# A parallel FNet and gated layer in split fp32: the odd block and the rest rows of the last stage join the 2x2 scheme as a twelfth pair

## The chip, the cores and the metric

The kernel runs on one core of one Trainium2 chip. The metric is the time of one execution on the device, in microseconds (us). Three runs of the kernel before gave a median of 1033.83 us (1033.81 to 1034.27).

## What is computed

The reference, cut to what matters (S = 2048 tokens, D = 640, F = 1728, all fp32):

```python
xn = _layernorm(x, axis=-1)
# A: FNet mixing
a = einsum("bsd,ed->bse", xn, dft_hid_re);  b = einsum("bsd,ed->bse", xn, dft_hid_im)
A = einsum("ts,bse->bte", dft_seq_re, a) - einsum("ts,bse->bte", dft_seq_im, b)
# B: gated layer
gate = einsum("bsd,df->bsf", xn, W_gate);  up = einsum("bsd,df->bsf", xn, W_up)
h = where(gate > 0, gate, 0) * up
return x + A + einsum("bsf,fd->bsd", h, W_down)
```

## The kernel before, in words

Every fp32 operand is split into a high part (a copy rounded to the fp32r format, by ScalarE) and a low part (the rest, by VectorE; `split`, L123), and every product of two operands is made of three matmuls, high x high, high x low and low x high, into one PSUM bank (`mm3`, L127).

The kernel has three stages. In the first, the sequence transforms of the normalized tokens are made first (the order of the two transforms in A is exchanged), as partial products P and Q that go to DRAM (`pqd`). In the second, 26 rounds (`gate_up`, 13 blocks of 128 columns of F for each half of the tokens, some 12 us a round) make h and store it to DRAM (`hd`, 13 blocks of 128 rows for each half; `hrest`, the 64 rows that are left, since 1728 = 13 x 128 + 64). In rounds 13 to 23, `pair_weights` (L945) prepares beside that the weights of the last stage and stores them in DRAM as `wparts`. The third stage, `project` (L1038), which the change is about, adds everything up: out = x + hid x (P, Q) + W_down x h, transposed, so that 128 outputs stand in the partitions and 512 tokens in the columns.

The last stage runs over two halves of the tokens (q = 1, then 0), each of two chunks of 512 tokens. A half's product is made by a 2x2 scheme of seven products instead of eight (Strassen's scheme in Winograd's form): the inner dimension is cut into pairs of 128-row blocks, the outputs into pairs of blocks (0, 1 against 2, 3; the fifth block of outputs goes along in the products that allow it), the tokens into the two chunks. The seven products of a half follow each other in the order B11, T1, B21, T2, B22, T3, T4. The T's take differences of the loaded chunks as moving operand (VectorE makes them, L1092 to L1104) and prepared sums as weights. B11, T1, B21 and B22 write three output tiles each, T2, T3 and T4 two: 18 tiles. Each product runs over 11 pairs of blocks in six units: h0, h1 (two pairs each) and h2 (one pair) over the hidden dimension (P against Q), f0, f1, f2 (two pairs each) over blocks 0 to 11 of h. So a unit of two pairs is 18 matmuls in a product with three tiles, and 12 in one with two. A product's result is read out of its PSUM banks by VectorE, which adds it to a tile y (`add_y`, L1192); y starts as x, loaded by L1190, and goes to DRAM when its last product has been added. T2, T3 and T4 add to the banks "a" of the products before them: B11 writes a, T2 adds, T3 adds, T4 adds, with a read after each.

Block 12 of h and the 64 rest rows do not make a pair. Before the change they are done by plain products (`plain_block` L1128, `plain_rest` L1147, `plain_run` L1174): ten tiles in a half, each by three matmuls for block 12 and two for the rest rows, which stand twice in the partitions, so that one matmul does two of the three partial products. They run behind B21 and B22 (three tiles each) and behind T3 (two tiles of banks "o" of their own, then two of the banks a).

The order of the work: units are entered in a list `todo` of (load, prepare, run, finish) and `drive(4, 2)` (L701) walks through it: a unit's loads are issued four entries ahead of its matmuls, its splits two ahead, its read one behind. Loads are all issued from SP's queue in this order, so a load that waits holds up every load behind it; output stores are issued by GpSimd's queue, except the last ones. The pools set the waits: `ring2` (3 buffers for the split moving operand), `wraw` (4 raw weight tiles), `wts` (5 split weight tiles; for T2, T3 and T4 the loads go right into these, L1075), `raws` (24 raw chunks of 4 KB in a partition; each lives until the last product that needs it), `plain`, and `y` (ten tiles of 2 KB). The pools are opened where the ones of the earlier stages were closed (L1035), some from the left and some from the right end of the memory, and a new tile waits for the tiles that lay in its place.

The first unit of the stage (h0 of B11, q = 1) is made ahead, so that TensorE goes over without a break: its operands are loaded by `lead_load` and split by `lead_split` into a tile of the second stage's weight pool gw1 (L989 to L1000), which also held the weights of the last round. This is the lead unit; in the profile its matmuls are `ps<-gw`. Its raw chunk is loaded once more into `raws` (L1068 and L1069), as T1 needs it. In the profile `rw` is a raw chunk, `wr` a raw weight tile, `cb` a split chunk, `wt` a split weight tile, `pw` the tile of `pair_weights`, and `hp`, `hr`, `wp`, `wq`, `pr` are the plain products' tiles.

Of the kernel before, what the change touches and what calls it, by code (L numbers as in the profile page):

```python
# [7 lines left out]
F32 = mybir.dt.float32  # L8
# [43 lines left out]
NPAIR = KD + NF // 2  # L52
# [6 lines left out]
def fnet_reglu_kernel(  # L59
# [885 lines left out]
    def pair_weights(k, n):  # L945

        t = {}

        def load():
            t["z"] = z = pool("prep").tile([P, Y12 + 2 * P], F32, name="pw")  # L950
            wa, wb = pair(k, 1)
            for w, o1, o2 in ((wa[0], Y11, Y21), (wb[0], Y12, LOW + Y22)):
                nc.sync.dma_start(z[:, o1 : o1 + 2 * P], w[:, : 2 * P])
                nc.sync.dma_start(z[:, o2 : o2 + 2 * P], w[:, 3 * P :])

        def prepare():
# [3 lines left out]
            tt(zz(LOW + Z2), zz(Z1), zz(Y11), op=OP.subtract)  # L960
            tt(zz(LOW + Z3), zz(Y11), zz(Y21), op=OP.subtract)
            tt(zz(Z4), zz(Y12), zz(LOW + Z2), op=OP.subtract)

            high, src = z[:, HIGH:LOW], z[:, LOW:NW]
            split(high.bitcast(F32R), src, src)

        loads[n - 1].append(load)
        besides[n].append(prepare)
        issues[n + 1].append(lambda: nc.gpsimd.dma_start(wparts[:, k], t["z"][:, :NW]))

    def pair(k0, n):

        if k0 < KD:
            return hid[0, k0 : k0 + n], hid[1, k0 : k0 + n]
        f = 2 * (k0 - KD)
        w = wd[f * P : (f + 2 * n) * P].rearrange("(k i p) n -> k i p n", i=2, p=P)
        return w[:, 0], w[:, 1]
# [57 lines left out]
    for n, b, side in (("wraw", 4, "left"), ("ring2", 3, "left"), ("wts", 5, "left"), ("raws", 24, "left"), ("plain", 1, "right"), ("y", 1, "right")):  # L1035
        open_pools[n] = ctx.enter_context(tc.tile_pool(name=n, bufs=b, side=side, reuse_waits="tile"))

    def project(q):  # L1038
        c0, c1 = 2 * q, 2 * q + 1
        units = [("hid", u) for u in HID_UNITS] + [("f", u) for u in F_UNITS]  # L1040
        raws, B, y, plain = {}, {}, {}, {}

        def get(kind, u):
            what, ks = units[u]
            o = raws[kind, u] = pool("raws").tile([P, 2, CH], F32, name="rw")[:, : len(ks)]
            col, row = int(kind in ("B12", "B22")), int(kind in ("B21", "B22"))
            if what == "hid":
                nc.sync.dma_start(o, pqd[(c0, c1)[col]][row][:, ks[0] : ks[-1] + 1])
            else:
                nc.sync.dma_start(o, hd[q][2 * ks[0] + row : 2 * ks[-1] + row + 1 : 2, :, col * CH : (col + 1) * CH].rearrange("f p t -> p f t"))  # L1050

        def unit(name, u, first):
            what, ks = units[u]
            n, k0 = len(ks), ks[0] + (KD if what == "f" else 0)
# [3 lines left out]
            def load():  # L1058
# [6 lines left out]
                ahead = {("B21", 1): 0, ("B21", 3): 1, ("B21", 5): 2, ("T2", 0): 3, ("T2", 2): 4, ("T2", 3): 5}.get((name, u))  # L1065
# [4 lines left out]
                own, sums = [i.rearrange("k p n -> p k n") for i in pair(k0, n)], wparts[:, k0 : k0 + n]  # L1070
                if name in PARTS:
                    t["w"] = w = weights()
                    for j in range(n):
                        at = sums[:, j, HIGH:].rearrange("p (v n) -> p v n", v=2)[:, :, PARTS[name] : PARTS[name] + 2 * P]
                        nc.sync.dma_start(w[:, j, :, : 2 * P].bitcast(F32), at)  # L1075
                    return
# [8 lines left out]
            def prepare():  # L1085
# [5 lines left out]
                with in_turn():  # L1091
# [3 lines left out]
                    elif name == "T2":  # L1095
                        src = r("B12")
                        sub(src, r("B22"), src)
                    elif name == "T3":
                        src = r("B11")
                        sub(src, r("B12"), src)  # L1100
                    elif name == "T4":

                        src = r("B21")
                        sub(src, src, r("B12"))  # L1104
# [3 lines left out]
                    lows.append(split(b[:, 0], b[:, 1], src))  # L1108
                    if "r" in t:
# [3 lines left out]
            def run():  # L1113
# [5 lines left out]
                for out, oo, more in [((key, i), o + i * P, more) for i in range(2)] + ([(row4[1], row4[0], name in ("B21", "B22"))] if row4 else []):  # L1119
                    if first and not more:  # L1120
                        B[out] = bank()
                    for j in range(n):
                        mm3(B[out], (w[:, j, 0, oo : oo + P], w[:, j, 1, oo : oo + P]), (b[:, 0, j], b[:, 1, j]),
                            first and not more and j == 0, u == len(units) - 1 and j == n - 1, more)

            return load, prepare, run

        def plain_block():  # L1128


            def load():
                plain["r"] = r = pool("plain").tile([P, W2 + D], F32, name="pr")
                nc.sync.dma_start(r[:, :W2], hd[q][NF - 1])
                if q == 1:
                    nc.sync.dma_start(r[:, W2:], wd[(NF - 1) * P : NF * P])

            def prepare():
                r = plain["r"]
                plain["h"] = h = pool("plain").tile([P, 2, W2], F32R, name="hp")
                split(h[:, 0], h[:, 1], r[:, :W2])  # L1140
                if q == 1:
                    PW["w"] = w = pool("plain").tile([P, 2, D], F32R, name="wp")
                    split(w[:, 0], w[:, 1], r[:, W2:])

            todo.append((load, prepare, idle, idle))

        def plain_rest():  # L1147


            def load():  # L1150
                plain["r2"] = r = pool("plain").tile([P, W2 + D], F32, name="pr")
                for i in range(2):
                    at = slice(i * REST, (i + 1) * REST)
                    nc.sync.dma_start(r[at, :W2], hrest[q])
                    if q == 1:
                        nc.sync.dma_start(r[at, W2:], wd[NF * P :])

            def prepare():
                r = plain["r2"]
                plain["hr"] = h = pool("plain").tile([P, W2], F32R, name="hr")  # L1160
                high = pool("plain").tile([P, W2], F32R, name="hh")
                a, b = slice(0, REST), slice(REST, 2 * REST)
                copy(h[a], r[a, :W2])
                split(high[b], h[b], r[b, :W2])
                if q == 1:

                    PW["wr"] = w = pool("plain").tile([P, 2, D], F32R, name="wq")
                    for i in range(2):
                        at = slice(i * REST, (i + 1) * REST)
                        split(w[at, i], w[at, 1 - i], r[at, W2:])  # L1170

            todo.append((load, prepare, idle, idle))

        def plain_run(tiles):  # L1174
            for key, e, c in tiles:
                new = key not in B
                if new:
                    B[key] = bank()
                cs, es = slice(c * CH, (c + 1) * CH), slice(PLACE[e] * P, (PLACE[e] + 1) * P)
                (w, wr), (h, hr) = (PW["w"], PW["wr"]), (plain["h"], plain["hr"])  # L1180
                mm3(B[key], (w[:, 0, es], w[:, 1, es]), (h[:, 0, cs], h[:, 1, cs]), new, False, not new)
                for v in range(2):
                    nc.tensor.matmul(B[key], wr[:, v, es], hr[:, cs], start=False, stop=v == 1, skip_group_check=not new)  # L1183
# [17 lines left out]
        def reading(name):  # L1201
# [21 lines left out]
        for name in ("B11", "T1", "B21", "T2", "B22", "T3", "T4"):  # L1223

            tiles = {"B21": [(("c", i), i, 0) for i in range(2)] + [("v1", 4, 0)],
                     "B22": [(("b", i), i, 1) for i in range(2)] + [("v2", 4, 1)],
                     "T3": [(("o", i), 2 + i, 1) for i in range(2)]}.get(name)
            for u in range(len(units)):
                l, p, r = unit(name, u, u == 0)
                end = u == len(units) - 1 and not (tiles and name != "T3")  # L1230
# [3 lines left out]
                if name == "B21" and u in (0, 2):  # L1234
                    (plain_rest if u else plain_block)()
            if tiles:
                todo.append((idle, idle, (lambda t: lambda: plain_run(t))(tiles),
                             (lambda n: lambda: read(n))("own" if name == "T3" else name)))
            if name == "T3":
                todo.append((idle, idle, lambda: plain_run([(("a", i), 2 + i, 0) for i in range(2)]), idle))  # L1240

    PW, PARTS = {}, {"T2": Z2, "T3": Z3, "T4": Y22}
# [43 lines left out]
```

## Time and profile before

| | |
|---|---|
| median of three runs | 1033.83 us (1033.81 to 1034.27) |
| the profiled execution | 1033.63 us, of which the span from the first to the last instruction 1031.9 |
| TensorE matmuls | 1024.6 us, 4528 instructions |
| VectorE, ScalarE, GpSimd | 801.1, 430.1 and 117.3 us busy |
| moved by DMA | 242.73 MB, mean 235 GB/s |
| the last stage | from 737.3 us (its first unit, the lead, from about 733) to the end |
| mean granted TensorE clock | 1.000 |

How to read the views: in a timeline a row has the start in the span, the duration in us, the engine (SPq is SP's queue of loads), the line of the kernel, the operation, out<-in and the shape; in square brackets, how long the engine was idle ahead of it and what ended that. A row of waits has the waiting line, what it waited for, the sum in us, how often, and the longest. A row of transfers has the tiles, the queue, the count, the size and the median time from issue to landing. A row of windows has the window, its length, then for TensorE, its weight loads, VectorE, ScalarE and GpSimd the busy time with the count, then the granted clock, the DMA engines' busy share and GB/s.

### The profile page before, as it was taken

How to read it: one execution, taken by the hardware profiler on the slowest of the kernel's cores; microseconds unless marked ns; L12 is line 12 of the kernel's file. 1: busy time of each engine (PE TensorE's matmuls, PEld its weight loads, DVE VectorE, ACT ScalarE, POOL GpSimd, SP SyncE). 2: the span in 40 equal slices, each digit the busy share in tenths (PEclk: the TensorE clock that was granted, in tenths of full speed). 3: DMA queues.
4: the chain of work that ended last, by engine and by line, in shares of the span. 5: the costliest groups of instructions: out<-in, count | busy, mean ns of one | idle time of the engine just before them, and what ended most of it. 6: DMA issues, size and time to landing. Idle time of an engine off the chain costs nothing.

```text
span 1031.9 us, 12494 instructions
## 1 busy us (share of the span) xinstructions
PE 1024.6 (99%) x4528; PEld 844.7 (82%) x4528; DVE 801.1 (78%) x1074; ACT 430.1 (42%) x544; POOL 117.3 (11%) x184
## 2 busy tenths in 40 slices
PE   9999999999999999999999999999999999999998
PEld 7878888888888888888888888888778888888886
DVE  7777887998989576788878988886497667886764
ACT  6654453343443333433335443443365423552521
POOL 3431001012110002321110001000000000000000
PEclk9999999999999999999999999999999999999999
DMA  8878734867968885763364665662798637986543
GB/s 307 304 266 301 261 132 167 328 234 242 372 236 314 319 308 169 253 217 133 145 246 148 221 234 215 228 256 102 240 341 294 195 126 227 377 304 214 159 154 122
DMA packets 101469, 242.73 MB, mean 235 GB/s; under 512 B 11552, under 2 KB 50976, under 8 KB 98848
## 3 DMA queue, kind: packets, MB, share of 16 engines
q1 hardware_dynamic: 83664, 171.68, 48.6%
q0 software_dynamic: 17744, 70.26, 18.3%
q8 instruction: 35, 0.57, 0.2%
q14 instruction: 26, 0.21, 0.1%
HBM read 182.12 MB, written 58.74 MB: 233 GB/s over the span
## 4 chain that ended last, share of the span: by engine, by line
PE 96%; DVE 2%; DMA 1%; ACT 1%; issue 0%; SPq 0%; DVEq 0%; ACTq 0%
PE ps L132 31%; PE ps L131 31%; PE ps L130 31%; PE ps L471 3%; PE ps L1183 1%; DMA rw<-hd 1%; DVE bs L204 0%; DMA r<-in_x 0%; ACT xs_late L261 0%; ACT xs_early L261 0%; ACT mv L212 0%; DVE mv L205 0%; DVE r L265 0%; DVE cb L125 0%; SPq L1190 0%
## 5 line engine op out<-in xcount | busy, mean ns | idle before, releaser
L130 PE MATMUL ps<-cb,wt 128*128 128x512 f32 x390 | 151.9, 390 | 0.6 <-ACT wt L124 0.6
L132 PE MATMUL ps<-cb,wt 128*128 128x512 f32 x390 | 151.9, 390 | 0.4 <-DVE wt L125 0.4
L131 PE MATMUL ps<-cb,wt 128*128 128x512 f32 x390 | 151.8, 389 | 0.0
L125 DVE TENSOR_TENSOR cb<-rw,cb 128x1024 fp32r<-128x1024 f32 x83 | 93.9, 1132 | 70.8 <-ACT cb L124 70.1
L124 ACT ACTIVATE cb<-rw 128x1024 fp32r<-128x1024 f32 x83 | 82.0, 988 | 151.7 <-PE ps L132 127.3
L124 ACT ACTIVATE cb<-raw 128x1024 fp32r<-128x1024 f32 x71 | 75.3, 1061 | 123.0 <-PE ps L132 106.3
L125 DVE TENSOR_TENSOR cb<-raw,cb 128x1024 fp32r<-128x1024 f32 x71 | 86.7, 1222 | 35.7 <-ACT cb L124 35.5
L130 PE MATMUL ps<-xs_early,gw 128*128 128x512 f32 x260 | 101.2, 389 | 0.0
L131 PE MATMUL ps<-xs_early,gw 128*128 128x512 f32 x260 | 101.2, 389 | 0.0
L132 PE MATMUL ps<-xs_early,gw 128*128 128x512 f32 x260 | 101.1, 389 | 0.0
L130 PE MATMUL ps<-cb,xs_late 128*128 128x512 f32 x232 | 90.2, 389 | 0.0
L131 PE MATMUL ps<-cb,xs_late 128*128 128x512 f32 x232 | 90.2, 389 | 0.0
L132 PE MATMUL ps<-cb,xs_late 128*128 128x512 f32 x232 | 90.2, 389 | 0.0
L121 ACT ACTIVATE gw<-z 128x1024 fp32r<-128x1024 f32 (+1 forms) x52 | 57.6, 1109 | 76.4 <-DVE z L793 76.4
L130 PE MATMUL ps<-cb,xs_early 128*128 128x512 f32 x226 | 87.9, 389 | 0.0
L131 PE MATMUL ps<-cb,xs_early 128*128 128x512 f32 x226 | 87.9, 389 | 0.0
L132 PE MATMUL ps<-cb,xs_early 128*128 128x512 f32 x226 | 87.9, 389 | 0.0
L130 PEld LDWEIGHTS ps<-cb,wt 128*128 128x128 f32 x390 | 73.2, 188 | 16.2 <-ACT wt L124 1.0
L132 PEld LDWEIGHTS ps<-cb,wt 128*128 128x128 f32 x390 | 73.2, 188 | 15.8 <-DVE wt L125 0.7
L131 PEld LDWEIGHTS ps<-cb,wt 128*128 128x128 f32 x390 | 73.2, 188 | 15.6 <-DVE cb L125 0.3
L121 ACT ACTIVATE u<-ps 128x512 f32<-128x512 f32 x52 | 31.1, 597 | 94.4 <-PE ps L132 94.4
L803 DVE TENSOR_TENSOR gw<-z,gw 128x1024 fp32r<-128x1024 f32 (+1 forms) x52 | 64.6, 1282 | 3.8 <-ACT gw L121 3.8
(197 smaller groups left out, 1981.0 us busy)
## 6 DMA issues: line engine op xcount, KB each, us to landing
raw<-in_dft SPq DMA_DIRECT2D x94, 512.0 KB, 5.5
wt<-wparts SPq DMA_DIRECT2D x66, 256.0 KB, 3.2
z<-in_wgu SPq DMA_DIRECT2D x26, 640.0 KB, 3.9
hd<-ob POOLq DMA_DIRECT2D x26, 512.0 KB, 3.7
rw<-hd SPq DMA_DIRECT2D x24, 512.0 KB, 6.6
wparts<-pw POOLq DMA_DIRECT2D x11, 1024.0 KB, 4.1
tk<-in_dft SPq DMA_DIRECT2D x16, 512.0 KB, 6.7
set<-r POOLq DMA_DIRECT2D x16, 512.0 KB, 3.3
```

The source lines that it names most:

```text
L121: return nc.scalar.activation(o, i, AF.Copy)
L124: nc.scalar.activation(hi, src, AF.Copy)
L125: return nc.vector.tensor_tensor(lo, src, hi.bitcast(F32), op=OP.subtract)
L130: nc.tensor.matmul(ps, wh, mh, start=first, stop=False, skip_group_check=more)
L131: nc.tensor.matmul(ps, wh, ml, start=False, stop=False, skip_group_check=more)
L132: nc.tensor.matmul(ps, wl, mh, start=False, stop=last, skip_group_check=more)
L471: start["pe"] = pin([nc.tensor.matmul(E[0, key], xn_part(n * SG + j, d)[v == 1], b[:, int(v == 2), j], start=False, stop=n % NH == NH - 1 ...
L803: tt(self.w[:, 1, cs], self.z[:, cs], self.w[:, 0, cs].bitcast(F32), op=OP.subtract)
L1183: nc.tensor.matmul(B[key], wr[:, v, es], hr[:, cs], start=False, stop=v == 1, skip_group_check=not new)
```

## The change

Block 12 of h and the 64 rest rows become a twelfth pair, a seventh unit "end" of each product, and the plain products go. The second block of that pair has only 64 rows. Where a product needs the pair's first block or a difference or sum with it (B11, T1, T2, T3), the unit is done as the others are, by three matmuls a tile. Where its operands have only 64 rows (B21, B22, T4: "short" in the code), the rows are put twice into the 128 partitions, the weights as high and low part, the moving operand as high part twice; one matmul over 128 rows then does two of the three partial products, and one over 64 rows the third. So the twelfth pair has 3 matmuls in 10 tiles and 2 in 8 tiles of a half.

With it:
- `pair_weights` prepares and stores a twelfth pair, in round 24 of the second stage; GpSimd writes zeros into the half of the weight tile that no row fills.
- `raws` has 28 buffers instead of 24; pool `plain` is gone, and the pool `y` is now the only one at the right.
- B22's raw chunk of the new unit is filled up with zeros by GpSimd, since T2 takes a difference over all 128 rows.
- In T4 the new unit is the last but one; in the other products it is the last.
- T3 is now read behind its last unit and its y tiles are stored then; before, its plain part was in other banks, which were read and stored separately.

The diff, cut to its core:

```diff
-NPAIR = KD + NF // 2
+NPAIR = KD + NF // 2 + 1
...
-            wa, wb = pair(k, 1)
-            for w, o1, o2 in ((wa[0], Y11, Y21), (wb[0], Y12, LOW + Y22)):
-                nc.sync.dma_start(z[:, o1 : o1 + 2 * P], w[:, : 2 * P])
-                nc.sync.dma_start(z[:, o2 : o2 + 2 * P], w[:, 3 * P :])
+            wa, wb = (w[0] for w in pair(k, 1))
+            if wb.shape[0] < P:
+                for o in (Y12, LOW + Y22):
+                    nc.gpsimd.memset(z[REST:, o : o + 2 * P], 0.0)
+            for w, o1, o2 in ((wa, Y11, Y21), (wb, Y12, LOW + Y22)):
+                nc.sync.dma_start(z[: w.shape[0], o1 : o1 + 2 * P], w[:, : 2 * P])
+                nc.sync.dma_start(z[: w.shape[0], o2 : o2 + 2 * P], w[:, 3 * P :])
...
-    for n, b, side in (("wraw", 4, "left"), ("ring2", 3, "left"), ("wts", 5, "left"), ("raws", 24, "left"), ("plain", 1, "right"), ("y", 1, "right")):
+    for n, b, side in (("wraw", 4, "left"), ("ring2", 3, "left"), ("wts", 5, "left"), ("raws", 28, "left"), ("y", 1, "right")):
...
-        units = [("hid", u) for u in HID_UNITS] + [("f", u) for u in F_UNITS]
+        units = [("hid", u) for u in HID_UNITS] + [("f", u) for u in F_UNITS] + [("end", (NF // 2,))]
...
+            elif what == "end" and row:
+                if col:
+                    nc.gpsimd.memset(o[b2], 0.0)
+                nc.sync.dma_start(o[a, 0], hrest[q][:, col * CH : (col + 1) * CH])
...
+            short = what == "end" and name in ("B21", "B22", "T4")
...
-                ahead = {("B21", 1): 0, ("B21", 3): 1, ("B21", 5): 2, ("T2", 0): 3, ("T2", 2): 4, ("T2", 3): 5}.get((name, u))
+                ahead = {("B21", 1): 0, ("B21", 3): 1, ("B21", 5): 2, ("T2", 0): 3, ("T2", 2): 4, ("T2", 3): 5, ("T2", 4): 6}.get((name, u))
...
+                    if short:
+                        copy(b[b2, 0], src[a])
+                        lows.append(split(b[a, 0], b[a, 1], src[a]))
+                    else:
+                        lows.append(split(b[:, 0], b[:, 1], src))
+                    if "r" in t and short:
+                        t["w"] = w = weights()
+                        copy(w[:, :, 0], t["r"])
+                        sub(w[b2, :, 0], t["r"][b2], w[b2, :, 0].bitcast(F32))
...
+                    if short:
+                        nc.tensor.matmul(B[out], w[:, 0, 0, oo : oo + P], b[:, 0, 0], start=False, stop=False, skip_group_check=more)
+                        nc.tensor.matmul(B[out], w[a, 0, 0, oo : oo + P], b[a, 1, 0], start=False, stop=last, skip_group_check=more)
+                        continue
...
-        def plain_block():
...
-        def plain_rest():
...
-        def plain_run(tiles):
...
-                return [(2 + i, 1, ("a", i), False) for i in two]
-            if name == "own":
-                return [(2 + i, 1, ("o", i), "late") for i in two]
+                return [(2 + i, 1, ("a", i), True) for i in two]
...
-            for u in range(len(units)):
-                l, p, r = unit(name, u, u == 0)
-                end = u == len(units) - 1 and not (tiles and name != "T3")
+            us = list(range(len(units)))
+            if name == "T4":
+                us[-2:] = us[:-3:-1]
+            for u in us:
+                end = u == us[-1]
+                l, p, r = unit(name, u, u == 0, end)
```

More of the change, by code (lines that the diff above doesn't have):

```diff
@@ L1039, in project @@
         c0, c1 = 2 * q, 2 * q + 1
-        units = [("hid", u) for u in HID_UNITS] + [("f", u) for u in F_UNITS]
-        raws, B, y, plain = {}, {}, {}, {}
+        units = [("hid", u) for u in HID_UNITS] + [("f", u) for u in F_UNITS] + [("end", (NF // 2,))]
+        raws, B, y = {}, {}, {}
+        a, b2 = slice(0, REST), slice(REST, 2 * REST)
         def get(kind, u):
@@ L1101, in prepare @@
                     elif name == "T4":
-                        src = r("B21")
-                        sub(src, src, r("B12"))
+                        src, at = r("B21"), a if short else slice(0, P)
+                        sub(src[at], src[at], r("B12")[at])
                     else:
@@ L1121, in run @@
                         B[out] = bank()
+                    if short:
+                        nc.tensor.matmul(B[out], w[:, 0, 0, oo : oo + P], b[:, 0, 0], start=False, stop=False, skip_group_check=more)
+                        nc.tensor.matmul(B[out], w[a, 0, 0, oo : oo + P], b[a, 1, 0], start=False, stop=last, skip_group_check=more)
+                        continue
                     for j in range(n):
                         mm3(B[out], (w[:, j, 0, oo : oo + P], w[:, j, 1, oo : oo + P]), (b[:, 0, j], b[:, 1, j]),
-                            first and not more and j == 0, u == len(units) - 1 and j == n - 1, more)
+                            first and not more and j == 0, last and j == n - 1, more)
@@ L1126, in unit @@
             return load, prepare, run
-        def plain_block():
[L1131 to L1145, printed above, removed]
@@ L1147, in plain_rest @@
-        def plain_rest():
[L1150 to L1172, printed above, removed]
@@ L1174, in plain_run @@
-        def plain_run(tiles):
[L1175 to L1183, printed above, removed]
@@ L1233, in project @@
                     todo.append(((lambda name: lambda: get_y(name))(name), idle, idle, idle))
[L1234 to L1242, printed above, removed]
+    PARTS = {"T2": Z2, "T3": Z3, "T4": Y22}
     for q in (1, 0):
```

27 lines of the change are left out of this document (19 added, 8 removed).

## The prediction

> **What bounds the kernel now.** I read the page first (busy shares, chain of work that ended last), then the waits of TensorE in the last stage, then TensorE, the load queue SP and the splits in order of time.
>
> ```profile
> span 1031.9 us, 12494 instructions
> ...
> PE 1024.6 (99%) x4528; PEld 844.7 (82%) x4528; DVE 801.1 (78%) x1074; ACT 430.1 (42%) x544; POOL 117.3 (11%) x184
> ...
> PE 96%; DVE 2%; DMA 1%; ACT 1%; issue 0%; SPq 0%; DVEq 0%; ACTq 0%
> ```
>
> TensorE is busy all through and carries the chain, so time moves only where matmuls go or where TensorE stops. The waits of TensorE after 735 us are two:
>
> ```profile
> PE ps L130 <- ACT wt L124: 0.6, 1, 0.6
> PE ps L132 <- DVE wt L125: 0.4, 1, 0.4
> ```
>
> ```profile
> 737.07 0.39 PE L132 MATMUL ps<-gw 128*128 128x512 f32 x1
> 737.29 0.39 PE L130 MATMUL ps<-cb,wt 128*128 128x512 f32 x1
> ...
> 747.27 0.39 PE L132 MATMUL ps<-cb,wt 128*128 128x512 f32 x1
> 748.28 0.50 PE L130 MATMUL ps<-cb,wt 128*128 128x512 f32 x1 [0.62 <-ACT wt L124]
> 748.80 0.49 PE L131 MATMUL ps<-cb,wt 128*128 128x512 f32 x1
> 749.67 0.50 PE L132 MATMUL ps<-cb,wt 128*128 128x512 f32 x1 [0.37 <-DVE wt L125]
> 750.01 0.39 PE L130 MATMUL ps<-cb,wt 128*128 128x512 f32 x1
> ```
>
> From 737.29 to 747.27 there are 44 steps (units h1, h2, f0 of B11: 18+9+18 matmuls): 9.98/44 = **0.227 us a matmul**; the 0.39 overlap. From 747.27 to 750.01 are 4 steps, 0.91 at that pace; the stage's only stall costs 2.74-0.91 = **1.83 us**. Its cause is on SP:
>
> ```profile
> 726.36 0.33 SPq L1048 DMA_DIRECT2D rw<-pq  x1
> 726.73 0.43 SPq L1079 DMA_DIRECT2D wr<-in_hid  x1
> ...
> 728.67 0.47 SPq L1079 DMA_DIRECT2D wr<-in_wd  x1
> 737.49 1.29 SPq L1190 DMA_DIRECT2D y<-in_xt  x3
> 738.83 0.43 SPq L1050 DMA_DIRECT2D rw<-hd  x1
> ```
>
> After the loads up to f0, SP stands still until 737.49: the y tiles lie where the lead unit's operands lie (tile gw1), and the last lead matmul starts at 737.07. f1's loads queue behind, and come late.
>
> **The change, part by part.** The sum starts from the profiled execution, 1033.63 us (1.73 outside the span; the median of three runs is 1033.83).
>
> *Matmuls.* Removed: per half 10 plain tiles of 5 matmuls, 50. Added: the twelfth pair in 18 tiles; B11, T1, T2, T3 write 10 of them by three matmuls, B21, B22, T4 write 8 by two: 46. Over both halves 8 fewer: **-1.81 us**. The trace has no 64-row matmul; 16 are added. From nothing to one restart (0.50) each they would change this by -3.6 to +4.4; I take 0.227, the 512 columns of the nearest row.
>
> *Where the buffers lie.* In the built kernel the y tiles move up into the place of the token sets, which the gate/up rest has read before the lead unit starts: their wait goes, and f1's loads no longer queue behind it. **-1.83 us**, unless something else is late; and something is. With 28 raw slots instead of 24 the upper ones reach into gw1. The first raw tile takes the lowest slot, the second (B11, h0, needed only by T1) the highest, inside gw1. In the built order that load waits for the count of the last lead matmul, and behind it in SP's queue stand everything else: h1's weights, h2, f0, the y tiles, f1. The load that was issued at 726.36 is issued at 737.49, 11.13 later.
>
> ```profile
> wr<-in_hid SPq DMA_DIRECT2D x1, 384.0 KB, 4.1
> ```
> ```profile
> 747.40 0.83 ACT L124 ACTIVATE wt<-wr 128x768 fp32r<-128x768 f32 x1
> ```
> ```profile
> 748.67 0.95 DVE L125 TENSOR_TENSOR wt<-wr,wt 128x768 fp32r<-128x768 f32 x1
> ```
>
> h1's weights were issued 0.37 behind and landed after 4.1 us. So they land at 737.49+0.37+4.1 = 741.96; ScalarE's high part takes 0.83, VectorE's low part 0.95, each hand-over 0.04: third matmul of h1 at 743.87. It would start at 737.29+2 x 0.227 = 737.74. With 0.11 for the slower restart (749.67 to 750.01 is 0.34) the new stall is **+6.25 us**. Bounds, with the page's row of what the DMA engines moved in 40 slices:
>
> ```profile
> GB/s 307 304 266 301 261 132 167 328 234 242 372 236 314 319 308 169 253 217 133 145 246 148 221 234 215 228 256 102 240 341 294 195 126 227 377 304 214 159 154 122
> ```
>
> Were both loads (0.917 MB) moved at the best slice's 377 GB/s, without any start, they would be there after 2.4 us instead of 4.5: a stall of 4.2. With the 6.5 us that the same load takes in the other half (below) it is 8.65.
>
> Do the next units stall again? Each load waits for the landing of the one eight places ahead. f0's weights, last of the burst, and f1's weights took:
>
> ```profile
> wr<-in_wd SPq DMA_DIRECT2D x1, 384.0 KB, 7.2
> ```
> ```profile
> wr<-in_wd SPq DMA_DIRECT2D x1, 384.0 KB, 8.0
> ```
>
> f0: 728.67+11.13+7.2 = 747.0, split by 749.4 with its moving part ahead in both queues; its third matmul, 27 after h1's, is due at 750.1. f1: its weights wait for h2's raw tile (about 742.8), land at 750.8, are split by 752.7, and are due at 754.2. Nothing added, 0.7 to spare; a landing 1 us slower costs 0.3.
>
> *T3 to T4.* T4 adds into the banks that T3 filled, and they must first be read. Before, ten plain matmuls of other banks (2.27 us) covered the read. Now T4 follows T3 directly.
>
> ```profile
> 1025.84 0.39 PE L132 MATMUL ps<-cb,wt 128*128 128x512 f32 x1
> ```
> ```profile
> 1026.27 0.69 DVE L1193 TENSOR_TENSOR y<-ps,y 128x512 f32<-128x512 f32 x1 [4.43 <-PE ps L132]
> ```
>
> The first bank's last matmul stands 4 steps (0.91) ahead of T4's first; the read starts 0.43 behind it, takes 0.69, hand-over 0.05: 1.17-0.91 = 0.26 per half. The second bank is covered, since the built order puts five matmuls of h1 between. VectorE is close to late there:
>
> ```profile
> 1003.10 0.68 DVE L1089 TENSOR_TENSOR rw<-rw 128x512 f32<-128x512 f32 x1
> 1003.77 1.22 DVE L125 TENSOR_TENSOR cb<-rw,cb 128x1024 fp32r<-128x1024 f32 x1
> 1004.91 1.22 DVE L1089 TENSOR_TENSOR rw<-rw 128x1024 f32<-128x1024 f32 x1
> 1006.49 1.22 DVE L125 TENSOR_TENSOR cb<-rw,cb 128x1024 fp32r<-128x1024 f32 x1 [0.36 <-ACT cb L124]
> ```
>
> A full unit of T3 gives VectorE two steps of 1.14 for 2.72 us of TensorE (12 matmuls), the short unit two of up to 0.67 for 1.36. One step behind costs 1.14 more. **+0.6 us** for both halves; bounds 0.5 and 2.8. The same counting leaves 0.5 us in T2, where the short unit's difference waits also for GpSimd's zeroing, queued behind three output stores; no row shows a zeroing. GpSimd's mean operation is 117.3/184 = 0.64 us. I take nothing; beyond the 0.5 it costs what it is late.
>
> *T4 to the second half.* T4's order (h0, h1, h2, f0, f1, end, f2) makes its last weights wait for h1's release, not h0's, and the next half's loads stand behind them.
>
> ```profile
> 861.89 8.19 SPq L1075 DMA_DIRECT2D wt<-wparts  x4
> 870.12 0.47 SPq L1048 DMA_DIRECT2D rw<-pq  x1
> 870.63 0.43 SPq L1079 DMA_DIRECT2D wr<-in_hid  x1
> ```
> ```profile
> wr<-in_hid SPq DMA_DIRECT2D x1, 384.0 KB, 6.5
> ```
> ```profile
> 879.00 1.23 DVE L125 TENSOR_TENSOR cb<-rw,cb 128x1024 fp32r<-128x1024 f32 x1
> ```
> ```profile
> 866.27 0.39 PE L130 MATMUL ps<-cb,wt 128*128 128x512 f32 x1
> ```
> ```profile
> 881.48 0.39 PE L131 MATMUL ps<-cb,wt 128*128 128x512 f32 x1
> ```
>
> T4's 66 matmuls start at 866.27 and the next half's first at 881.25 (0.227 before the row shown); the next half's second matmul (881.48) needs the split that ends at 880.23: 1.20 to spare with 0.05 hand-over. The loads come 12 matmuls (2.72) later, T4 ends 4 (0.91) later: 1.81-1.20 = **+0.6 us**; bounds 0 and 1.6.
>
> *At nothing.* Preparing the twelfth pair (four sums, a split with the 0.95 and 0.83 above) falls in round 24 of the gate/up stage, where VectorE idles about half the time and ScalarE more:
>
> ```profile
> L960 DVE TENSOR_TENSOR pw<-pw x11: 424/425/427, 577.3 to 697.9; 128x256 f32<-128x256 f32 x11
> ```
> ```profile
> 710.00:720.00 10.00, 10.00 (x46) 8.28 (x45) 5.13 (x6) 1.92 (x4) 0.53 (x1) 1.00 0.12 50
> ```
>
> Without that cover: 2.6 us. The removed plain splits and loads stood beside TensorE, which never waited for them; the end (last read, last store) stays.
>
> **Sum:** 1033.63-1.81-1.83+6.25+0.6+0.6 = **1037.4 us**.
>
> **The rivals.**
>
> *The clock drops in the new gap.* TensorE would stand still from about 737.5 to 742.9. For it: nothing here has stood as long. Against it: the granted clock (the 1.00 ahead of the DMA share 0.23) is full already at the first matmuls.
>
> ```profile
> 1.00:2.00 1.00, 0.97 (x10) 0.97 (x11) 0.00 (x0) 1.00 (x1) 0.00 (x0) 1.00 0.23 41
> ```
> ```profile
> 1.03 4.79 PE L112 MATMUL ps<-warm 128*128 128x128 bf16 x48 [1.03 <-DVE warm L108]
> ```
>
> These 128-column matmuls step at 0.10 us, 0.40 for 512 columns. For as long as they run (4.79 us) 12 matmuls would do instead of 21: at most 2.1 us. **1039.5 us** at that price. The Trainium skill, page "TensorE: Matmul & The Clock Gate", section "Part 1: The HAM clock gate (the "warmup" mystery)", speaks for this rival: an idle window of about 3.4 us halves the clock until about as long has been busy. By that rule half a clock for 3.4 us would cost 1.7 us (an estimate from the page); the first row does not show the lower clock after the idle start, and the 1.83 us stall was too short to tell.
>
> *Slow landings.* The burst lands as in the second half (6.5 for 4.1): +2.4, **1039.8 us**.
>
> *Fast landings.* The burst finds idle queues and lands at the bound of 2.4 us: -2.1, **1035.3 us**, within what a measurement tells. Against it: the burst of 726.36 found idle queues too.
>
> *The other side: the wait is not the lead unit's.* gw1 was first used by round 25's weights. If the second raw load is held only by these, it issues at 726.36 again, nothing is late, and 1033.63-1.81-1.83+0.6+0.6 = **1031.2 us**. It decides at 733.7: issued earlier than 6.25-2.44 = 3.8 us ahead of 737.49, the load leaves the kernel no slower than before. For it: SP's second load did start there. Against it: the y tiles, in the same place, waited until 737.49.
>
> **How the numbers follow.** Forecast 0.56, clock 0.18, slow landings 0.11, fast landings 0.09, other side 0.06. The range, 1034.7 to 1040.5, leaves out the other side, and the outermost of clock and slow landings together. Forecast, clock and slow landings are slower by over 0.2% (2.07 us, about what a measurement of this kernel can tell): 0.85; fast landings within: 0.09; other side faster: 0.06.
>
> **What would show it.** Right: the second rw load issued at about 737.5, TensorE waiting for h1's weights some 5.4 us and not for f1's, 0.3 us at each start of T4 waiting for a read of y, a short wait at the second half's start, eight matmuls fewer. Wrong: SP loads at 726 as before; stalls at T2's or T3's short unit or at the zeroing; a clock below 1.00.

## The result and the profile after

The changed kernel takes 1045.35 us (median of four runs, 1044.94 to 1045.69) against 1033.82 us (four runs, 1032.41 to 1034.27): a ratio of 1.0117, 95% interval 1.0105 to 1.0129. It is slower by 11.5 us. The forecast was 1037.4 us, and the range ended at 1040.5: the sign was right, the size was not. The profiled execution took 1045.69 us, its span is 1043.9, 12.0 us more than before.

The page of the changed kernel, its busy times and the shares of the chain that ended last:

```profile
span 1043.9 us, 12622 instructions
...
PE 1031.7 (99%) x4520; PEld 844.0 (81%) x4520; DVE 812.8 (78%) x1098; ACT 439.0 (42%) x564; POOL 120.6 (12%) x191
...
PE 94%; DVE 2%; DMA 1%; ACT 1%; issue 1%; SPq 0%; POOL 0%; DVEq 0%; ACTq 0%; POOLq 0%
```

TensorE has 8 matmuls fewer and is busy for 7.1 us longer. So the waits cannot be the whole story: matmuls themselves became slower somewhere. The waits of TensorE in the last stage:

```profile
PE ps L130 <- ACT wt L124: 5.4, 1, 5.4
PE ps L131 <- DVE cb L125: 0.7, 1, 0.7
PE ps L130 <- issue: 0.3, 2, 0.2
```

These are the three waits that were forecast (h1's weights, the second half's start, the two starts of T4), and no other. The wait for f1's weights is gone. Now the four places one by one. First SP's queue, then TensorE at the lead unit's end:

```profile
719.43 18.60 SPq L1054 DMA_DIRECT2D rw<-pq  x2
738.08 0.43 SPq L1104 DMA_DIRECT2D wr<-in_hid  x1
...
740.52 1.77 SPq L1170 DMA_DIRECT2D y<-in_xt  x3
```
```profile
737.28 0.39 PE L132 MATMUL ps<-gw 128*128 128x512 f32 x1
743.09 0.80 PE L130 MATMUL ps<-cb,wt 128*128 128x512 f32 x1 [5.42 <-ACT wt L124]
743.68 0.63 PE L131 MATMUL ps<-cb,wt 128*128 128x512 f32 x1
744.11 0.77 PE L132 MATMUL ps<-cb,wt 128*128 128x512 f32 x1
...
747.24 0.50 PE L130 MATMUL ps<-cb,wt 128*128 128x512 f32 x1
747.58 0.40 PE L131 MATMUL ps<-cb,wt 128*128 128x512 f32 x1
```

The two raw loads at L1054 stand as one row of 18.60 us, since the second waits until after 737.28, the last lead matmul; h1's weights follow at 738.08. The gap at h1 is 743.09-737.28-0.227 = 5.58 us, and h1's third matmul starts at 744.11, where 743.87 was forecast. But behind the gap the ten steps (a step is the time from one matmul's start to the next) from 743.09 to 747.58 take 4.49 us instead of 2.27. The granted clock of the windows (the third number from the end of each row) says why:

```profile
740.50:741.00 0.50, 0.00 (x0) 0.00 (x0) 0.00 (x0) 0.00 (x0) 0.00 (x0) 0.64 0.97 364
741.00:741.50 0.50, 0.00 (x0) 0.00 (x0) 0.00 (x0) 0.00 (x0) 0.00 (x0) 0.50 1.07 397
...
747.00:747.50 0.50, 0.50 (x3) 0.40 (x2) 0.50 (x1) 0.50 (x1) 0.00 (x0) 0.54 0.98 324
747.50:748.00 0.50, 0.50 (x3) 0.41 (x3) 0.50 (x1) 0.19 (x1) 0.00 (x0) 1.00 0.98 352
```

The clock falls to half in the gap, at about 740.64 (0.64 in that half microsecond is 0.14 us at 1.00 and 0.36 at 0.50), and is full again from about 747.46. The slow steps cost 4.49-2.27 = 2.22 us. (The first three of them wait in part for h1's low part, which VectorE ends at 744.03; the forecast counted that in its gap.) Second, a short unit (L1156 is its 128-row matmul, L1157 the 64-row one), with the weight loads and the clock of the same stretch:

```profile
812.67 0.39 PE L1156 MATMUL ps<-cb,wt 128*128 128x512 f32 x1
812.99 0.50 PE L1157 MATMUL ps<-cb,wt 64*128 64x512 f32 x1
813.41 0.49 PE L1156 MATMUL ps<-cb,wt 128*128 128x512 f32 x1
...
815.46 0.39 PE L131 MATMUL ps<-cb,wt 128*128 128x512 f32 x1
```
```profile
812.45 0.19 PEld L1156 LDWEIGHTS ps<-cb,wt 128*128 128x128 f32 x1
812.99 0.18 PEld L1157 LDWEIGHTS ps<-cb,wt 64*128 64x128 f32 x1 [0.35 <-issue]
813.41 0.19 PEld L1156 LDWEIGHTS ps<-cb,wt 128*128 128x128 f32 x1 [0.25 <-issue]
```
```profile
812.00:814.00 2.00, 2.00 (x8) 1.08 (x6) 0.77 (x2) 1.06 (x1) 0.00 (x0) 1.00 0.39 124
```

The seven steps from 812.67 to 815.46 take 2.79 us instead of 1.59. A step of 0.43 again, but this time at a clock of 1.00. The weight loads tell the cause: the 128-row one at 812.45 runs 0.22 ahead of its matmul, beside the matmul before; each load behind a change of row count starts only with its own matmul, after 0.25 to 0.35 of idle put down to "issue". In the units of B21 and B22 that is 1.20 us each, in T4's (five steps in 1.94 instead of 1.13) 0.81: 2 x (1.20+1.20+0.81) = 6.4 us in the kernel. None of it appears in the list of waits.

Third, the start of T4, with the read that it waits for, and fourth, the second half's second matmul:

```profile
872.64 0.39 PE L132 MATMUL ps<-cb,wt 128*128 128x512 f32 x1
873.19 0.47 PE L130 MATMUL ps<-cb,wt 128*128 128x512 f32 x1 [0.17 <-issue]
873.50 0.39 PE L131 MATMUL ps<-cb,wt 128*128 128x512 f32 x1
```
```profile
872.41 0.68 DVE L1173 TENSOR_TENSOR y<-ps,y 128x512 f32<-128x512 f32 x1
```
```profile
889.98 0.40 PE L130 MATMUL ps<-cb,wt 128*128 128x512 f32 x1
891.07 0.50 PE L131 MATMUL ps<-cb,wt 128*128 128x512 f32 x1 [0.69 <-DVE cb L125]
891.40 0.39 PE L132 MATMUL ps<-cb,wt 128*128 128x512 f32 x1
```

Two steps of 0.86 instead of 0.45: 0.40 at each T4, the read's end at 873.09 in front of it. And 1.42-0.45 = 0.97 at the second half. The sum over the stage:

| | forecast, us | in the trace of after, us |
|---|---|---|
| eight matmuls fewer | -1.81 | -1.81 |
| the wait for f1's weights | -1.83 | -1.83 |
| the gap at h1 | +6.25 | +5.58 |
| slow steps behind the gap, at half clock | (a rival) | +2.22 |
| changes between 128 and 64 rows | 0 | +6.4 |
| T3 to T4 | +0.6 | +0.8 |
| T4 to the second half | +0.6 | +0.97 |
| sum | +3.8 | +12.3, of 12.0 between the spans |

The forecast measured its gap at h1's third matmul, with 0.11 us for a slow restart. Measured in the same way the trace has 744.11-737.28-3 x 0.227 = 6.15, and 0.11, which is the forecast's 6.25; of the 7.80 us in the two rows 1.5 are then left for the clock.

### The profile page after: what moved, and what is told of

Same layout as the page of the kernel before. It is cut to its first block, busy times and chain, and to the rows that moved or that the text cites. A ratio compares the mean times of both kernels' runs of the same rounds, so it can differ in the third digit from the quotient of the medians.

```text
span 1043.9 us, 12622 instructions
## 1 busy us (share of the span) xinstructions
PE 1031.7 (99%) x4520; PEld 844.0 (81%) x4520; DVE 812.8 (78%) x1098; ACT 439.0 (42%) x564; POOL 120.6 (12%) x191
## 4 chain that ended last, share of the span: by engine, by line
PE 94%; DVE 2%; DMA 1%; ACT 1%; issue 1%; SPq 0%; POOL 0%; DVEq 0%; ACTq 0%; POOLq 0%
PE ps L130 30%; PE ps L132 30%; PE ps L131 30%; PE ps L471 2%; DMA wr<-in_hid 1%; DVE bs L204 1%; PE ps L1157 1%; PE ps L1156 0%; DVE cb L125 0%; DVE r L265 0%; DMA r<-in_x 0%; ACT cb L124 0%; ACT xs_late L261 0%; DVE mv L205 0%; ACT mv L212 0%
## 5 line engine op out<-in xcount | busy, mean ns | idle before, releaser
L130 PE MATMUL ps<-cb,wt 128*128 128x512 f32 x410 | 161.3, 394 | 5.8 <-ACT wt L124 5.4
L131 PE MATMUL ps<-cb,wt 128*128 128x512 f32 x410 | 160.3, 391 | 0.7 <-DVE cb L125 0.7
L132 PE MATMUL ps<-cb,wt 128*128 128x512 f32 x410 | 160.1, 391 | 0.0
L124 ACT ACTIVATE cb<-rw 128x1024 fp32r<-128x1024 f32 (+2 forms) x97 | 90.7, 936 | 138.8 <-PE ps L132 98.3
L125 DVE TENSOR_TENSOR cb<-rw,cb 128x1024 fp32r<-128x1024 f32 (+2 forms) x97 | 102.9, 1068 | 57.7 <-ACT cb L124 57.6
L130 PEld LDWEIGHTS ps<-cb,wt 128*128 128x128 f32 x410 | 77.5, 189 | 24.3 <-ACT wt L124 5.8
L131 PEld LDWEIGHTS ps<-cb,wt 128*128 128x128 f32 x410 | 77.5, 189 | 16.9 <-DVE cb L125 1.1
L132 PEld LDWEIGHTS ps<-cb,wt 128*128 128x128 f32 x410 | 77.3, 189 | 16.5 <-DVE wt L125 0.5
```

The costliest lines, as they stand in the source:

```text
L124: nc.scalar.activation(hi, src, AF.Copy)
L125: return nc.vector.tensor_tensor(lo, src, hi.bitcast(F32), op=OP.subtract)
L130: nc.tensor.matmul(ps, wh, mh, start=first, stop=False, skip_group_check=more)
L131: nc.tensor.matmul(ps, wh, ml, start=False, stop=False, skip_group_check=more)
L132: nc.tensor.matmul(ps, wl, mh, start=False, stop=last, skip_group_check=more)
```

## The experiments

Theory A: of what the forecast missed, about 6.4 us are paid at the changes between 128-row and 64-row matmuls, and 2.2 us to a clock that the gap itself has lowered. The rivals: a 64-row matmul is slow by itself; the short units are late for their splits; the slow matmuls behind the gap come from the traffic of that moment; the gap has another cause than the raw slot. The ratio in each heading is to the kernel before, whose median was 1033.2 to 1033.5 us beside them.

**e1_grouped: 1043.19 us, 1.0101 (1.0075 to 1.0126).**

```diff
     if short:
         matmul(B[out], w[:, 0, 0, ...], b[:, 0, 0], ...)
-        matmul(B[out], w[a, 0, 0, ...], b[a, 1, 0], ...)
+        later.append((out, oo, more))
...
+for out, oo, more in later:
+    matmul(B[out], w[a, 0, 0, ...], b[a, 1, 0], ...)
```

> The changed kernel with one thing moved: in a short unit (B21, B22, T4) the 128-row matmuls of all its tiles come first and the 64-row ones behind them, instead of alternating; so 2 changes of row count in a unit instead of 6 (three tiles) or 4 (two tiles). Theory A (each CHANGE of row count costs about 0.2 us, since the weight load then no longer runs beside the matmul before it): 6.3 us of price falls to 6 units x 2 x 0.195 = 2.3, so about 1041.4 us instead of 1045.35, and 64-row matmuls behind each other step at 0.227. Rival B (a 64-row matmul is dear by itself, whatever stands beside it): nothing changes, 1045.3, and the 64-row matmuls step at 0.43.

The same unit of TensorE's timeline in this kernel (L1157 the 128-row, L1164 the 64-row matmuls, three in a row):

```profile
813.35 0.84 PE L1157 MATMUL ps<-cb,wt 128*128 128x512 f32 x3
814.12 0.96 PE L1164 MATMUL ps<-cb,wt 64*128 64x512 f32 x3
815.01 0.50 PE L130 MATMUL ps<-cb,wt 128*128 128x512 f32 x1
815.35 0.40 PE L131 MATMUL ps<-cb,wt 128*128 128x512 f32 x1
```

The seven steps take 2.00 us, 0.41 too much instead of 1.20, and so in each of the six units: two changes at 0.2 us. From 814.12 to 815.01 three steps take 0.89, that is 3 x 0.227 and one change: 64-row matmuls behind each other are not slow. Theory A stands for the price, and the rival falls. The time came down by 2.2 us where the steps gave 3.9, since other losses grew: in this run the gap was 5.84 us with 12 slow steps behind it (0.7 us more together), and short waits for split chunks came in B22's first unit (0.7 us over both halves).

**e2_full_rows: 1041.82 us, 1.0075 (1.0058 to 1.0091).**

```diff
-        matmul(B[out], w[a, 0, 0, ...], b[a, 1, 0], ...)
+        matmul(B[out], w[:, 0, 0, ...], b[:, 1, 0], ...)
...
     copy(b[b2, 0], src[a])
+    nc.scalar.activation(b[b2, 1], src[a], AF.Copy, scale=0.0)
```

> The changed kernel with the second matmul of each short tile done over all 128 rows; ScalarE writes zeros into the 64 rows of the moving operand that were left out (6 more instructions of about 0.5 us). The count of matmuls, the weights and the order are the same. Theory A (the price is the change of row count): no extra in the short units, 1045.35 - 6.3 = 1039.1 us. Rival (the short units are late for another reason, their half-height splits or weights): about 1045, with the same 0.427 steps or waits in their place.

The extra in the short units is gone altogether, with as many matmuls; but the time fell by 3.5 us, not by 6.3. The waits of TensorE in this kernel tell where the rest is:

```profile
PE ps L130 <- ACT wt L124: 5.7, 1, 5.7
PE ps L131 <- DVE cb L125: 1.8, 3, 0.8
PE ps L130 <- DMA wt<-wparts: 0.4, 1, 0.4
PE ps L130 <- issue: 0.3, 2, 0.2
```

Where the changed kernel waited once for a split chunk, this one waits three times (also at B22's first unit, in both halves) and once for T2's weights. By the steps that costs 2.4 us more than in the changed kernel, most of what is missing. The slow steps had given the loads time: a loss that goes uncovers one that it hid.

**e3_own_pool: 1037.23 us, 1.0036 (1.0024 to 1.0048).**

```diff
-("raws", 28, "left"), ("y", 1, "right")
+("raws", 24, "left"), ("y", 1, "right"), ("rawe", 4, "right")
...
-pool("raws").tile([P, 2, CH], ...)
+pool("rawe" if what == "end" else "raws").tile([P, 1 if what == "end" else 2, CH], ...)
```

> The changed kernel with the raw chunks of the new unit in a pool of their own (4 buffers of 2 KB at the right, where the token sets lay), and the pool of raw chunks back at 24 buffers, so that no raw slot reaches into the lead unit's tile. Theory A (the second raw load waits for that tile, and the 2.3 us of slow matmuls behind the gap come from the gap): both go, 1045.35 - 5.6 - 2.3 = 1037.5 us. Rival 1 (the slow matmuls have another cause, such as traffic of the loads): 1039.8. Rival 2 (the wait has another cause than the slot): about 1045.

SP's queue in this kernel, the second raw load, h1's weights behind it, and the y loads:

```profile
726.41 0.33 SPq L1054 DMA_DIRECT2D rw<-pq  x1
726.80 0.43 SPq L1104 DMA_DIRECT2D wr<-in_hid  x1
...
733.21 1.37 SPq L1170 DMA_DIRECT2D y<-in_xt  x3
```

The second raw load is issued at 726.41, where it was at 726.36 before the change and at 737.70 in the changed kernel; TensorE goes through h1 and f1 without a wait, and the clock stays at 1.00. It saved 8.1 us, where 7.9 were expected. The slot was the cause, and with the gap the slow matmuls went.

**e5_filler: 1045.08 us, 1.0113 (1.0098 to 1.0128).**

```diff
+if name == "B11" and (q, u) == (1, 0):
+    for i in range(24):
+        matmul(B["a", 0], warm, (warm four times side by side), start=False, stop=False)
```

> The changed kernel with 24 matmuls that add zeros (the bf16 tile of the warm-up, 512 columns each, into the lead unit's first bank) between the lead unit and h1, so that TensorE has work through most of its 5.4 us gap; the waits and loads stay as they are. Theory A (the gap lowers the clock, and the matmuls of 743 to 747 step at 0.427 for that reason): the gap is still there, filled, and the steps behind it are 0.227: 1045.35 - 2.3 = 1043.1 us with a granted clock of 1.00 all through. Rival (they are slow because loads and splits run at that moment): still 0.427 behind the fillers, 1045.3.

TensorE in this kernel, at the fillers, h1 and f1:

```profile
737.49 5.35 PE L1164 MATMUL ps<-warm 128*128 128x512 bf16 x24
743.36 0.50 PE L130 MATMUL ps<-cb,wt 128*128 128x512 f32 x1 [0.52 <-ACT wt L124]
...
755.17 0.50 PE L132 MATMUL ps<-cb,wt 128*128 128x512 f32 x1 [0.36 <-DVE wt L125]
```

The same loads and splits run beside h1 as in the changed kernel, and the steps from 743.70 on are 0.227. (The first matmul that needs h1's low part comes sixth here instead of third, so it does not wait.) So the traffic is not the cause of the half clock, the idle time of TensorE is. The gain was smaller than expected. At full clock f1 comes up against its late weights and loses 1.1 us. The span is 1.5 us shorter than that of the changed kernel; the medians, 0.3 us apart with runs from 1044.2 to 1047.6, cannot tell it.

**e11_short_gap: 1045.45 us (one run), as e5_filler with 12 fillers.**

> e5_filler with 12 matmuls of zeros instead of 24, so that TensorE idles some 2.9 us ahead of h1 instead of 5.4 (the changed kernel) or 0.5 (e5_filler). If a gap of this length lowers the clock: steps of 0.427 behind it and a granted clock of 0.5. If it must be longer (the Trainium skill, page "TensorE: Matmul & The Clock Gate", section "Part 1: The HAM clock gate (the "warmup" mystery)", has a window of about 3.4 us): steps of 0.227 and a clock of 1.00. The time itself is read from the steps, not from this one run.

TensorE at h1 in this kernel, and the windows in which the clock turns:

```profile
743.12 0.50 PE L130 MATMUL ps<-cb,wt 128*128 128x512 f32 x1 [2.95 <-ACT wt L124]
```
```profile
744.50:745.00 0.50, 0.50 (x3) 0.44 (x2) 0.50 (x2) 0.00 (x0) 0.00 (x0) 0.66 1.05 393
...
748.00:748.50 0.50, 0.50 (x3) 0.37 (x3) 0.50 (x1) 0.00 (x0) 0.00 (x0) 0.93 1.06 397
```

In this run a gap of 2.95 us, with a wait of 0.26 us one matmul later, was enough. The clock falls at 744.66, 1.5 us after TensorE has work again, and is back at 748.07.

**e4_both: 1034.14 us, 1.0012 (1.0003 to 1.0021)**, the edits of e2 and e3 together. **e7_more_weights: 1031.54 us, 0.9995 (0.9983 to 1.0007)**, with two more tiles for prepared weights:

```diff
+("wtr", 2, "right")
...
-pool("wts").tile([P, 2, 2, 3 * P], ...)
+pool("wtr" if name in PARTS and u in (3, 6) else "wts").tile([P, 2, 2, 3 * P], ...)
```

> e2_full_rows and e3_own_pool together: no 64-row matmul, and no raw slot in the lead unit's tile. If each price goes as it went alone (3.5 us in e2, 8.1 in e3): 1045.35 - 3.5 - 8.1 = 1033.7 us, as the kernel before, with the waits of e2 left (a late split at the first unit of B22, about 1 us in a half). If the 64-row steps were paid in full and the waits of e2 came from the late start: 1037.2 - 6.3 = 1031.0.

> e4_both with two more tiles for the weights of T2, T3 and T4 (a pool of two at the right, for their units f0 and end), so that the load queue stands less behind them and the raw weights of B22 and of the second half are issued earlier. Theory A (the waits that came in e2 when the 64-row steps went are those of the load queue behind the five weight tiles): these waits go too, and the 64-row price shows in full: 1037.2 - 6.3 = 1031.0 us. Rival (they come from VectorE or ScalarE, which have as much to do as before): as e4_both.

e4 came out as the sum of the two edits one by one, with the late splits of e2 still there (three waits, 1.9 us). With the two tiles these waits go, and no wait of TensorE is left in the stage's list. So it was the load queue behind the weight tiles, not VectorE or ScalarE. From e3 to e7 the time falls by 5.7 of the 6.3 us. e7's median is 1.9 us below that of the kernel before; two of its ten runs took 4 to 5 us longer, so the interval reaches past 1.

**e8_read_covered: 1031.36 us, 0.9983 (0.9972 to 0.9993)**, and **e9_t3_order: 1037.08 us, 1.0034 (1.0021 to 1.0047)**, two ways to cover the read at T3's end, both from e7:

```diff
 # e8: f2 of T3 is held, and run with the new unit, tile by tile
+if name == "T3" and u == 5:
+    held["f2"] = w, b
+    continue
+if name == "T3" and u == 6:
+    (the six matmuls of f2 for this tile ahead of the three of "end")
...
 # e9: T3 in the order of T4
-if name == "T4":
+if name in ("T3", "T4"):
     us[-2:] = us[:-3:-1]
```

> e7_more_weights with T3's last two units run tile by tile (first tile: f2 and end, then second tile: f2 and end), so that the first bank is complete 9 matmuls ahead of T4's first instead of 3, and its read is covered. Theory A (the 0.40 at each start of T4 is the read of that bank): 0.8 us less than e7_more_weights, about 1030.2. Rival (the 0.40 is the price of any bank change there): the same as e7_more_weights.

> e7_more_weights with T3 in the order that T4 has already: the new unit is the last but one, the two-pair unit f2 the last. The first bank's last matmul then stands 7 steps (1.59 us) ahead of T4's first instead of 4, without a split operand that is held longer, as in e8_read_covered. Theory A (the 0.40 at each start of T4 is the read of that bank, 1.3 us from the last matmul to the end of the read): 0.8 us less than e7_more_weights, 1031.5 - 0.8 = 1030.7. Rival (the second half starts late again, as it did in e8_read_covered): 1031.5.

e8: at the two starts of T4, which cost 0.38 us each in e7, all steps are 0.227, so the loss was the read of the bank. But the spans are 1029.6 and 1029.7 us: T4's last unit now waits for its split, which stands behind a split of the second half's weights, and that gives 0.72 us back. e8 has the lowest median of all versions and is faster than the kernel before by 0.17%; its 0.2 us below e7 are too few to tell the two apart.

e9 was a miss. VectorE and TensorE of this kernel at the start of T4:

```profile
862.67 1.22 DVE L125 TENSOR_TENSOR cb<-rw,cb 128x1024 fp32r<-128x1024 f32 x1
863.80 0.68 DVE L1174 TENSOR_TENSOR y<-ps,y 128x512 f32<-128x512 f32 x1
```
```profile
864.59 0.47 PE L130 MATMUL ps<-cb,wt 128*128 128x512 f32 x1 [1.23 <-ACT cb L124]
```

The bank is complete earlier, but its read now stands behind a split of 1.22 us in VectorE's queue, so T4's first matmul comes 1.39 us late, where it came 0.30 late in e7. (The profile names ScalarE; its split ended at 864.08, the read at 864.48.) In T4's unit f1 two more waits came, 1.10 and 0.77 us with one matmul between them, and behind them half clock again:

```profile
877.50:878.00 0.50, 0.50 (x3) 0.43 (x2) 0.50 (x2) 0.50 (x2) 0.00 (x0) 0.61 1.08 414
...
881.00:881.50 0.50, 0.50 (x3) 0.38 (x2) 0.16 (x1) 0.26 (x1) 0.00 (x0) 0.97 1.03 395
```

**e10_row_halves: 1038.46 us, 1.0057 (1.0036 to 1.0079)**, from e9, so with its waits:

```diff
-        matmul(B[out], w[:, 0, 0, ...], b[:, 1, 0], ...)
+for i, (out, oo, more) in enumerate(later):
+    rows, v = ((a, 0), (b2, 1))[i % 2]
+    matmul(B[out], w[rows, 0, v, ...], b[rows, 1, 0], ...)
```

> e9_t3_order, but with 64-row matmuls again: in a short unit all 128-row matmuls first, then the 64-row ones, the second tile's in the upper 64 rows of the array and the others' in the lower (ScalarE makes the two copies that this needs). So 2 changes of row count in a unit (0.41 us by e1_grouped), 2.5 us in all. If 64-row matmuls in different halves of the rows run beside each other, one step of 0.227 goes in each of the 6 units: 1030.7 + 2.5 - 1.4 = 1031.8, and two of them start together. If they follow each other: 1033.2.

The three 64-row matmuls of B21's unit in this kernel:

```profile
806.60 0.73 PE L1167 MATMUL ps<-cb,wt 64*128 64x512 f32 x3
807.26 0.50 PE L130 MATMUL ps<-cb,wt 128*128 128x512 f32 x1
```

They and the change behind them take 0.66 us, 0.23 less than in e1: two of the three share one step. In three tiles what is shared so pays back about half of the two changes (0.41 in e1). The kernel is 1.4 us slower than e9 (1.1 expected), but the two times do not price it: e9 lost time at half clock, which this kernel did not, and this kernel has one more wait.

**e6_y_first: 1031.98 us, 0.9990 (0.9981 to 0.9999)**, the kernel before with one edit:

```diff
-("plain", 1, "right"), ("y", 1, "right")
+("y", 1, "right"), ("plain", 1, "right")
```

> The kernel before with one thing changed: its pool of y tiles is opened ahead of the pool of the plain products, so that y lies in the place of the token sets and not in the lead unit's tile. Theory A (the y loads held up the loads of f1, the stall of 1.83 us): they are issued at about 733 instead of 737.5, the stall goes, 1033.5 - 1.8 = 1031.7 us. Rival (the plain tiles, which now lie lower, take over the wait, or f1's weights land late anyway): 1033.5.

The y loads no longer wait for the last lead matmul, f1's loads follow right behind them, and no wait of TensorE is left in the stage. The time fell by 1.5 us of the 1.8. So the y tiles, and not the twelfth pair, bring most of what the repaired versions gain: e8's median is only 0.6 us below this kernel's.

## Why the prediction was right or wrong

- **The gap at h1 (+6.25): right in place, cause and size.** Its second raw load was held by the lead unit's tile, h1's third matmul came 0.24 us after the time given (the lead unit itself ended 0.21 later), the gap measured in the forecast's way is 6.15 against 6.13 without the restart, and e3 removed it by moving the slot alone. The rival that this load would go out at 726 did not happen.
- **f1's wait (-1.83): right.** e6 shows it by itself in the kernel before. "Nothing added" for f1 was right only because of the slow clock: in e5, with full clock, f1 does wait, 1.1 us, where 0.7 to spare had been counted.
- **T3 to T4 and the second half (+0.6 each): right in kind**, 0.8 and 0.97 measured, inside their bounds. That the second half's size is near is in part luck: its loads came 2.83 us later after T4's start, as counted (2.72), but the first weights took 7.5 us to land instead of 6.5, and T4 became 1.81 us longer instead of 0.91, since its changes of row count delayed the next half as well. The two misses nearly cancel.
- **The 64-row matmul: the step that failed.** "From nothing to one restart (0.50) each they would change this by -3.6 to +4.4; I take 0.227, the 512 columns of the nearest row." The nearest row was one without a change of row count. 16 of them cost 6.4 us above that, 0.40 each, and this lies outside the bound too, since one 64-row matmul between two 128-row ones makes two changes: the bound should have counted the matmul behind it as well. One source would have given the sign, though no price: the Trainium skill, "TensorEngine Tiling (Array Packing)", section "Key Properties", says that a change of the tiling mode drains TensorE, unlike a change of tile within a mode. e1 and e10 agree: 0.2 us for each change, nothing between 64-row matmuls.
- **The clock: a rival with 0.18 that came true.** Its price (at most 2.1 us) was about right: 2.22 us in the slow steps, 1.5 of them on top of the forecast's gap. What stood against it was misread. The window's 1.00 does not show that TensorE went at full pace at its first matmuls. Of the 48 warm-up matmuls in the kernel before, these are the first 37:

```profile
1.03 4.13 PE L112 MATMUL ps<-warm 128*128 128x128 bf16 x37 [1.03 <-DVE warm L108]
```

They take 4.13 us, 0.11 each; the other eleven take the 0.66 us that is left of the prediction's 4.79, 0.06 each. e5's fillers, at full clock, take 0.22 for four times the columns, which is 0.06 again. So TensorE did begin at about half pace after its idle start, and the 0.40 for 512 columns, with which the prediction priced the rival, was that pace. Read so, the prediction's two rows speak for the rival, and it deserved a larger chance than 0.18. The rule that the prediction cites from the Trainium skill pointed the same way.

Had the clock alone been added, the sum would have been 1037.4+1.5 = 1038.9, or 1039.6 with all of the 2.22 us, both still inside the range; the changes of row count alone put the time beyond it.

What stays open: why the read in e9 was placed behind the split, and whether e11's clock falls in each execution; it had one run.

## What to carry to other kernels

A matmul over half of the rows is not only a cheaper or equal matmul: count the changes of row count in the stream, put the half-row ones together and into both halves of the rows, or fill the rows with zeros. More buffers in a pool can cost more than they give when the new ones reach into memory that is still in use, since the first load into them holds up the whole queue behind it: look where each pool ends, not only whether it fits. And a stall is seldom priced alone: a long gap lowers the clock behind it, and a loss that is removed uncovers the next one.

## What the runs showed of the hardware

- Two alternating kinds of matmul (128 and 64 rows) step at 0.43 us instead of 0.227 at full clock, and the profile shows it neither as a wait of a matmul nor in the clock: only in the weight loads, which no longer run ahead.
- 64-row matmuls in the lower and the upper half of the rows, into different banks, ran beside each other: three in two steps (e10).
- The time at half clock came in pieces of one length: 740.64 to 747.46 is 6.82 us, twice 3.41, in the changed kernel, 744.66 to 748.07 is 3.41 in e11, 877.61 to 881.03 is 3.42 in e9. The Trainium skill, "TensorE: Matmul & The Clock Gate", section "Part 1: The HAM clock gate (the "warmup" mystery)", has free-running windows of 3413 ns, and these lengths agree.
- A fall did not need so long a time without any work. In the 3.41 us ahead of the fall TensorE was busy for 0.45 us in the changed kernel, for 1.27 in e11 and for 1.54 in e9, where two waits of 1.10 and 0.77 us had one matmul between them. With 2.8 us of work in such a stretch, on either side of 863.96 in e9 (the wait of 1.23 us at T4's start), the clock stayed at 1.00.
